# Hash-masked attention with a gated convolution: the sign products of heads 0 to 3 issued before the first scores, head 1 cast and stacked at once, one remainder of head 0 on GpSimd

## The chip, the cores and the metric

The kernel runs on one core of one Trainium2 chip. The metric is the device time of one execution in microseconds (us). Before the change the median of three runs is 633.61 us (633.21 to 634.43).

## The reference

```python
q_bits = (q @ proj > 0)                    # 6 bits for every row of q, and of k
k_bits = (k @ proj > 0)
q_bucket, k_bucket = sum(bits * 2**arange(6))
scores = where(q_bucket == k_bucket, q @ k.T / sqrt(D), -1e9)
attn = exp(scores - max(scores))           # per row
attn = attn / (sum(attn) + 1e-9)
x = (attn @ v), heads side by side         # B=4, H=8, S=768, D=64 -> (4, 768, 512)
gate = sigmoid(causal depthwise conv of x, 5 taps)
out = (gate * (x @ w_val)) @ w_out         # w: 512 x 512, given as float64
```

Batch 4, 8 heads, 768 rows, head dimension 64. The output is 4 x 768 x 512 in fp32.

## The kernel before

A *unit* is one of the 32 pairs of batch and head ("head i" below, heads 0 to 31 in order). A *tile* `k` is one block of 128 query rows of a head, six to a head, 192 in all; so tiles 0 to 5 belong to head 0, tiles 6 to 11 to head 1.

**Stacks.** fp32 products are made from parts that are rounded to fp32r. For each head there are four arrays: `aq` and `ak` (rounded q and k in rows 0 to 63, and in rows 64 to 75 the twelve sign rows that make the mask), `bq` and `bk` (128 rows that hold rounded values and remainders). `scores(k)` multiplies `ak` by `aq` and then `bk` by `bq` into one PSUM tile `s` (two halves of 384 columns, so four matmuls, L232). There are two `s` tiles, so `scores(k)` waits until `exponentials(k-2)` on ScalarE (ACT) has read its tile.

**Where the stacks come from.** The raw q and k of a head lie in `r` (`load_raw`, L147, five buffers). Head 0 goes a short way, `first_prep`: sign products into a PSUM tile `tp` (L211), casts on ACT and VectorE (DVE) (L213, L214, L215, L223), one remainder on GpSimd (POOL; L216: `bk`) and one on DVE (L217: `bq`), then four small evictions of the sign products on DVE (L219). All later heads go through `prep(i)`: GpSimd casts `aq` (L166) and subtracts for the remainder `bq` (L168); DMAs on SyncE's queue (SP) copy the rows to where they belong (L169 to L172) and the sign rows from a tile `u` (L174, L175). `u` holds the sign rows of four heads. `bits(i)` makes it in two halves: four small matmuls side by side in the columns of the array into a PSUM tile `m` (L194; one matmul for each of four heads, `raws[i + jj]`), and an eviction on DVE (L197). For heads 0 to 3 that is `first_bits`, a generator that is stepped, ahead of `prep(1)`, inside the main loop.

**The main loop** goes over `k`. In each turn stand, in this order: copies of the transposed probabilities of tile `k-4` out of PSUM (ACT, L289), `maxima(k)` (DVE, L238), small DVE steps (L244, L248, L262, L266), `normalise(k-2)` (GpSimd, L271), `scores(k+1)` (TensorE, PE), `exponentials(k)` (ACT, L256), steps of generators that run beside it (the preparation of the weights L90 to L112, the stacks `preps`, attention times v L303, the feed-forward part), and `transposes(k-3)` (PE, L280). Before the loop `scores(0)` is issued.

**What sets the order.** PE, ACT, DVE and GpSimd issue in the order in which the code is written (`manual_schedule`). The DMAs on SP are placed by a scheduler, and each waits on SP for what it needs, so a DMA that waits holds up those behind it. [...]

Of the kernel before, what the change touches and what calls it, by code (L numbers as in the profile page):

```python
# [8 lines left out]
FP32 = mybir.dt.float32  # L9
FP32R = mybir.dt.float32r  # L10
AF = mybir.ActivationFunctionType
ALU = mybir.AluOpType
# [14 lines left out]
def kernel(  # L27
# [10 lines left out]
    nc = tc.nc  # L38
    B, H, _, S = qk.shape
    P = 128  # L40
    D = 64
    KB = S // P
    HS = S // 2
# [9 lines left out]
    stk = ctx.enter_context(tc.tile_pool(name="stk", bufs=2))  # L53
# [9 lines left out]
    op = ctx.enter_context(tc.tile_pool(name="op", bufs=2))  # L63
# [3 lines left out]
    ps_v = ctx.enter_context(tc.tile_pool(name="ps_v", bufs=1, space=PSUM))  # L67
    ps_m = ctx.enter_context(tc.tile_pool(name="ps_m", bufs=1, space=PSUM))
# [5 lines left out]
    rows_sb = packed[:, 64:68]  # L74
    proj_sb = const.tile([P, 32], FP32, name="proj_sb")
# [67 lines left out]
    def load_raw(i):  # L143
        if i < len(units):
            b, h = units[i]
            raws[i] = raw.tile([P, S], FP32, name="r")
            nc.sync.dma_start(out=raws[i], in_=qk[b, h])  # L147

    def load_values(i):
        b, h = units[i]  # L150
        if h % 2 == 0:
            vts[i] = vp.tile([P, KB, P], FP32, name="vt")
            nc.sync.dma_start(out=vts[i], in_=v[b, h // 2])
        else:
            vts[i] = vts[i - 1]

    def prep(i):

        if i >= len(units):
            return  # L160
        b, h = units[i]
        j = h % 4
        load_values(i)
        r = raws[i]
        aq, ak, bq, bk = stacks[i] = [stk.tile([P, S], FP32R, name=nm) for nm in ("aq", "ak", "bq", "bk")]
        nc.gpsimd.tensor_copy(out=aq, in_=r)  # L166
        yield
        nc.gpsimd.tensor_tensor(out=bq, in0=r, in1=aq.bitcast(FP32), op=ALU.subtract)  # L168
        nc.sync.dma_start(out=ak[0:D].bitcast(FP32), in_=aq[D:P].bitcast(FP32))  # L169
        nc.sync.dma_start(out=bk[0:D].bitcast(FP32), in_=aq[D:P].bitcast(FP32))  # L170
        nc.sync.dma_start(out=bk[D:P].bitcast(FP32), in_=bq[D:P].bitcast(FP32))
        nc.sync.dma_start(out=bq[D:P].bitcast(FP32), in_=aq[0:D].bitcast(FP32))  # L172
        u = cur["u"]
        nc.sync.dma_start(out=aq[D:M].bitcast(FP32), in_=u[32 * j:32 * j + 2 * NB].bitcast(FP32))  # L174
        nc.sync.dma_start(out=ak[D:M].bitcast(FP32), in_=u[32 * j + 2 * NB:32 * j + 4 * NB].bitcast(FP32))  # L175
        load_raw(i + 5)
        if j == 3 and i + 1 < len(units):
            yield
            yield from bits(i + 1)

    def side_tile():
        if not moes:
            return ps_m.tile([P, 512], FP32, name="m")
        return ps_t.tile([P, 512], FP32, name="tp")

    def bits(i):

        u = stk.tile([P, S], FP32R, name="u", bufs=2)
        for hf in range(2):
            yield  # L190
            sl = slice(hf * HS, (hf + 1) * HS)
            z = side_tile()
            for jj in range(4):
                nc.tensor.matmul(out=z[32 * jj:32 * jj + 32, 0:HS], lhsT=proj_sb,  # L194
                                 rhs=raws[i + jj][:, sl], start=True, stop=True,
                                 tile_position=(0, 32 * jj))
            nc.vector.tensor_scalar(out=u[:, sl], in0=z[:, 0:HS], scalar1=rows_sb[:, 0:1], scalar2=rows_sb[:, 1:2],  # L197
                                    op0=ALU.is_ge, op1=ALU.mult)
        cur["u"] = u

    def first_bits():
        yield from bits(0)
        load_raw(5)

    def first_prep():

        r = raws[0]
        aq, ak, bq, bk = stacks[0] = [stk.tile([P, S], FP32R, name=nm) for nm in ("aq", "ak", "bq", "bk")]
        z = ps_t.tile([P, 512], FP32, name="tp")
        for g in range(4):  # L210
            nc.tensor.matmul(out=z[32 * g:32 * g + 2 * NB, 0:HS], lhsT=proj_sb[:, 2 * NB * (g // 2):2 * NB * (g // 2 + 1)],  # L211
                             rhs=r[:, HS * (g % 2):HS * (g % 2 + 1)], start=True, stop=True, tile_position=(0, 32 * g))
        nc.scalar.copy(out=aq[0:D], in_=r[0:D])  # L213
        nc.vector.tensor_copy(out=bk[D:P], in_=r[D:P])  # L214
        nc.vector.tensor_copy(out=ak[0:D], in_=r[D:P])  # L215
        nc.gpsimd.tensor_tensor(out=bk[0:D], in0=r[D:P], in1=bk[D:P].bitcast(FP32), op=ALU.subtract)  # L216
        nc.vector.tensor_tensor(out=bq[D:P], in0=r[0:D], in1=aq[0:D].bitcast(FP32), op=ALU.subtract)  # L217
        for g in (0, 2, 3, 1):
            nc.vector.tensor_scalar(out=(aq, ak)[g // 2][D:M, HS * (g % 2):HS * (g % 2 + 1)],  # L219
                                    in0=z[32 * g:32 * g + 2 * NB, 0:HS],  # L220
                                    scalar1=rows_sb[32 * g:32 * g + 2 * NB, 2:3],
                                    scalar2=rows_sb[32 * g:32 * g + 2 * NB, 3:4], op0=ALU.is_ge, op1=ALU.mult)
        nc.scalar.copy(out=bq[0:D], in_=r[0:D])  # L223

    def scores(k):
        i, qt = tiles[k]
        aq, ak, bq, bk = stacks[i]
        qs = slice(qt * P, (qt + 1) * P)
        s = ss[k] = ps_s.tile([P, 2, 512], FP32, name="s")
        for lq, rk, n in ((aq, ak, M), (bq, bk, P)):  # L230
            for hf in range(2):
                nc.tensor.matmul(out=s[:, hf, 0:HS], lhsT=lq[0:n, qs],  # L232
                                 rhs=rk[0:n, hf * HS:(hf + 1) * HS], start=n == M, stop=n == P)

    def maxima(k):
        s = ss[k]
        nm = small.tile([P, 1], FP32, name="nm")
        nc.vector.tensor_reduce(out=nm, in_=s[:, :, 0:HS], axis=AX.XY, op=ALU.max, negate=True)  # L238
        nms[k] = nm
# [182 lines left out]
    tiles = [(i, qt) for i in range(len(units)) for qt in range(KB)]  # L422

    raws, stacks, vts, ss, nbs, ps, tps, sums, rcs, nms, gs, cur = {}, {}, {}, {}, {}, {}, {}, {}, {}, {}, {}, {}
    avs, convs, moes = [], [], []
    accs = [(ps_m, "m")]

    def step(gens):

        while gens:  # L430
            try:
                return next(gens[0])
            except StopIteration:
                gens.pop(0)

    def finish(gens):
        while gens:
            step(gens)
# [3 lines left out]
    with tc.manual_schedule(engines=ENGINES):  # L442
        for i in range(5):
            load_raw(i)
        load_values(0)
        first_prep()
        weights = [[load_conv(), load_weights(0)], [load_weights(1)]]
        preps = [first_bits(), prep(1)]
        scores(0)
        step(weights[0])  # L450
        step(weights[1])
        turn = 0
        for k in range(N + LAG + 1):
            if 0 <= k - LAG - 1:
                keep_transposed(k - LAG - 1)
            pair = k % 2 == 0 and 0 <= k - 2 < N
            if k < N:
                maxima(k)
            if pair:
                row_sums(k - 2)  # L460
            if k < N:
                factors(k)
            if pair:
                recip(k - 2)
            if 0 <= k - 2 < N:
                normalise(k - 2)
            if k < N:
                shifts(k)
            if k + 1 < N:
                if tiles[k + 1][0] != tiles[k][0]:  # L470
                    finish(preps)
                    preps = [prep(tiles[k + 1][0] + 1)]
                scores(k + 1)
            if k < N:
                exponentials(k)
            if k >= 60 or k % 2:
                step(convs)
            for _ in range((1, 0, 2, 0, 2, 2)[k % 6]):
                step(weights[turn])
                turn = 1 - turn  # L480
            for _ in range(3 if cur["gates"] else 1):
                step(moes)
            cur["gates"] = max(0, cur["gates"] - 1)
            step(preps)
            if k % 2:
                step(avs)
                step(avs)
            if 0 <= k - LAG < N:
                transposes(k - LAG)
        accs[:] = [(ps_m, "m"), (ps_t, "tp"), (ps_s, "s"), (ps_t, "tp"), (ps_s, "s")]  # L490
        finish(avs)
        cur["gates"] = 0
        cur["end"] = True
        while convs:
            step(convs)
            step(moes)
        finish(moes)
# [59 lines left out]
```

## Time and profile before

| what | value |
|---|---|
| median of three runs | 633.61 us (633.21 to 634.43) |
| span of the profiled execution, from first to last instruction | 633.2 us |
| PE busy | 591.4 us (93%) |
| DVE busy | 451.3 us (71%) |
| ACT busy | 421.1 us (67%) |
| POOL busy | 386.0 us (61%) |
| mean granted TensorE clock | 0.986 |

The profile counts its times from the span's start; the median of the runs lies 0.4 us above that span. "Busy" counts every instruction of an engine; idle time of an engine that no one waits for costs nothing. In a timeline row stand: start in us, duration in us, engine, line, operation, written tile <- read tiles, shapes, how many instructions were merged, and in brackets the idle time just before and what ended it. "SPq" is a DMA being issued from SP; its transfer ends later.

### The profile page before, as it was taken

The page shows a single profiled execution, that of the slowest core. Times are in us where ns is not written, and L with a number is a line of the kernel's source. Part 1 is how long each engine was busy: PE and PEld are TensorE (multiplying, and loading weights), DVE is VectorE, ACT ScalarE, POOL GpSimd, SP SyncE. Part 2 cuts the span into 40 slices and gives each one's busy share as a digit, 9 for nine tenths or more (in the row PEclk, how much of TensorE's full clock was granted, in tenths as well). Part 3 has the DMA queues.
Part 4 walks back from the last instruction along what each step waited for, and adds up shares of the span by engine and source line. Part 5 has one row for each costly group of instructions (what it writes and reads, how often), then busy time and mean ns, then how long its engine had stood idle before and what let it go on. Part 6 is the DMA issues. An engine that isn't in the chain of part 4 may idle for free.

```text
span 633.2 us, 10639 instructions
## 1 busy us (share of the span) xinstructions
PE 591.4 (93%) x3496; PEld 426.2 (67%) x3496; DVE 451.3 (71%) x1033; ACT 421.1 (67%) x881; POOL 386.0 (61%) x357
## 2 busy tenths in 40 slices
PE   3699888989999999999999999999999999999997
PEld 2476555546667777676657777677667777776895
DVE  5689798999885856668675867668584786665532
ACT  3487777768778676667787776667778667675400
POOL 1476877778966765467754776467663677544221
PEclk9889997989999999999999999999999999999999
DMA  6533534443433334243333234243422223300111
GB/s 244 131 83 92 152 95 139 112 126 91 106 79 80 72 77 122 72 103 97 105 80 93 74 80 122 70 122 81 122 55 61 56 55 81 85 18 2 50 51 50
DMA packets 23270, 56.77 MB, mean 90 GB/s; under 512 B 4296, under 2 KB 4296, under 8 KB 23216
## 3 DMA queue, kind: packets, MB, share of 16 engines
q1 hardware_dynamic: 23072, 56.06, 33.3%
q8 instruction: 28, 0.46, 0.3%
q14 instruction: 26, 0.21, 0.1%
q10 hardware_dynamic: 144, 0.03, 0.0%
HBM read 23.12 MB, written 6.29 MB: 46 GB/s over the span
## 4 chain that ended last, share of the span: by engine, by line
PE 69%; ACT 14%; DVE 12%; issue 2%; DMA 2%; POOL 0%; SPq 0%; ACTq 0%; POOLq 0%; DVEq 0%
PE av L303 19%; PE s L232 17%; PE tp L280 12%; PE m L390 8%; PE m L365 7%; ACT p L256 6%; ACT pt L289 4%; DVE nm L238 3%; ACT x L311 3%; PE tp L365 1%; PE tp L390 1%; PE s L390 1%; DVE u L197 1%; PE tp L194 1%; DVE g L334 1%
## 5 line engine op out<-in xcount | busy, mean ns | idle before, releaser
L271 POOL TENSOR_SCALAR p<-p,ri 128x768 f32<-128x768 f32 x192 | 215.9, 1129 | 173.8 <-DVE nb L248 149.6
L238 DVE TENSOR_REDUCE nm<-s 128x1 f32<-128x768 f32 x192 | 182.5, 951 | 64.3 <-PE s L232 64.2
L289 ACT COPY pt<-tp 128x384 f32<-128x384 f32 x384 | 166.1, 485 | 86.7 <-PE tp L280 85.8
L256 ACT ACTIVATE p<-s,nb,gs 128x768 f32<-128x768 f32 x192 | 192.4, 1002 | 47.0 <-DVE nb L248 41.1
L280 PEld LDWEIGHTS tp<-ident,p 128*128 128x128 f32 x1152 | 131.2, 142 | 73.2 <-issue 46.4
L280 PE MATMUL tp<-ident,p 128*128 128x128 f32 x1152 | 166.3, 281 | 3.8 <-DVE u L197 1.5
L303 PE MATMUL av<-pt,vt 128*64 128x384 f32 x768 | 147.6, 506 | 0.0
L232 PE MATMUL s<-ak,aq 76*128 76x384 f32 x384 | 119.5, 393 | 28.9 <-ACT p L256 24.7
L232 PE MATMUL s<-bk,bq 128*128 128x384 f32 x384 | 101.6, 346 | 0.0
L303 PEld LDWEIGHTS av<-pt,vt 128*64 128x64 f32 x768 | 47.6, 137 | 63.7 <-issue 63.1
L232 PEld LDWEIGHTS s<-ak,aq 76*128 76x128 f32 x384 | 59.9, 196 | 45.2 <-ACT p L256 38.0
L334 DVE SCALAR_TENSOR_TENSOR g<-x,cw_sb,g 128x768 f32<-128x768 f32 x64 | 77.9, 1217 | 0.2
L232 PEld LDWEIGHTS s<-bk,bq 128*128 128x128 f32 x384 | 72.4, 195 | 0.5 <-issue 0.5
L376 POOL TENSOR_TENSOR hl<-ht,hh 128x384 fp32r<-128x384 f32 x32 | 32.2, 1006 | 45.9 <-DVE hh L374 45.9
L168 POOL TENSOR_TENSOR bq<-r,aq 128x768 fp32r<-128x768 f32 x31 | 58.3, 1882 | 0.0
L311 ACT COPY x<-av 64x384 f32<-64x384 f32 x64 | 30.3, 474 | 33.8 <-PE av L303 33.2
L365 PE MATMUL m<-xh,wv 128*128 128x384 f32 x200 | 42.8, 338 | 0.0
L248 DVE TENSOR_SCALAR nb<-nm,gs 128x1 f32<-128x1 f32 x192 | 39.9, 208 | 3.5
L324 POOL TENSOR_TENSOR xl<-x,xh 128x384 fp32r<-128x384 f32 x32 | 33.5, 1062 | 12.3 <-DVE xh L323 12.3
L370 DVE TENSOR_TENSOR ht<-m,g 128x384 f32<-128x384 f32 x25 | 13.9, 555 | 35.4 <-PE m L365 32.0
L256 ACT ACTIVATION_READ_ACCUMULATOR p<-s,nb,gs 128x1 f32 x192 | 39.0, 203 | 0.0
L390 PE MATMUL m<-wo,hh 128*128 128x512 f32 x144 | 38.2, 395 | 0.0
(84 smaller groups left out, 487.4 us busy)
## 6 DMA issues: line engine op xcount, KB each, us to landing
r<-in_qk_dram SPq DMA_DIRECT2D x32, 384.0 KB
vt<-in_v_dram SPq DMA_DIRECT2D x16, 384.0 KB
out_dram<-o SPq DMA_DIRECT2D x24, 256.0 KB
ak<-aq SPq DMA_DIRECT2D x31, 192.0 KB
bk<-aq SPq DMA_DIRECT2D x31, 192.0 KB
bk<-bq SPq DMA_DIRECT2D x31, 192.0 KB
bq<-aq SPq DMA_DIRECT2D x31, 192.0 KB
w<-in_w_val_dram SPq DMA_DIRECT2D x4, 512.0 KB
```

The source lines that it names most:

```text
L168: nc.gpsimd.tensor_tensor(out=bq, in0=r, in1=aq.bitcast(FP32), op=ALU.subtract)
L232: nc.tensor.matmul(out=s[:, hf, 0:HS], lhsT=lq[0:n, qs], rhs=rk[0:n, hf * HS:(hf + 1) * HS], start=n == M, stop=n == P)
L238: nc.vector.tensor_reduce(out=nm, in_=s[:, :, 0:HS], axis=AX.XY, op=ALU.max, negate=True)
L256: nc.scalar.activation(out=p, in_=s[:, :, 0:HS], func=AF.Exp, bias=nb, scale=gs.pop(k), accum_out=sm[:, k % 2, 0:1])
L271: nc.gpsimd.tensor_scalar(out=p, in0=p, scalar1=rcs.pop(k), scalar2=1.0, op0=ALU.mult, op1=ALU.mult)
L280: nc.tensor.transpose(out=tp[:, n * P:(n + 1) * P], in_=p[:, kb * P:(kb + 1) * P], identity=ident)
L289: nc.scalar.copy(out=pt[:, :, qo:qo + P], in_=tp[:, 0:HS].rearrange("p (a b) -> p a b", b=P))
L303: nc.tensor.matmul(out=av[s * D:(s + 1) * D, 0:HS], lhsT=vt[:, kb, hh * D:(hh + 1) * D], rhs=pt[kb // 3][:, kb % 3, :], start=(kb == 0), s ...
L311: nc.scalar.copy(out=x[hh * D:(hh + 1) * D, o:o + HS], in_=av[s * D:(s + 1) * D, 0:HS])
L334: nc.vector.scalar_tensor_tensor(out=g, in0=x[:, k:k + S], scalar=w, in1=g, op0=ALU.mult, op1=ALU.add)
L365: nc.tensor.matmul(out=acc[:, 0:HS], lhsT=wv[wi][:, c, j * P:(j + 1) * P], rhs=xs_[(c, o)][xi], start=(m == 0), stop=(m == 11))
L390: nc.tensor.matmul(out=acc, lhsT=hs[(o, j)][hi][:, tb * P:(tb + 1) * P], rhs=wo[wi][:, j, :], start=(m == 0), stop=(m == 11))
```

## The change

The change has four parts, all in the first turns of the program.

1. `first_bits` is gone. `first_signs` issues the sign matmuls of heads 0 to 3 right behind `first_prep` and ahead of `scores(0)`: the first half into the `m` tile, the second into the `av` tile. Both are evicted into `u` later, by DVE, inside `prep(1)`.
2. `prep(1)` no longer pauses between its cast and its remainder, and its first step is taken before the loop: GpSimd does both for head 1 ahead of the first `normalise`, and four copying DMAs are released. The DMAs of the sign rows still come after both evictions into `u`.
3. The remainder `bq[D:P]` of head 0 is computed on GpSimd in place of DVE.
4. `load_raw(5)` stands right behind `scores(0)`.

```diff
@@ prep(i) @@
         nc.gpsimd.tensor_copy(out=aq, in_=r)
-        yield
+        if i > 1:
+            yield
         nc.gpsimd.tensor_tensor(out=bq, in0=r, in1=aq.bitcast(FP32), op=ALU.subtract)
         ...
+        if i == 1:
+            yield
+            yield
+            for hf, z in enumerate(zs):
+                sl = slice(hf * HS, (hf + 1) * HS)
+                nc.vector.tensor_scalar(out=cur["u"][:, sl], in0=z[:, 0:HS], scalar1=rows_sb[:, 0:1],
+                                        scalar2=rows_sb[:, 1:2], op0=ALU.is_ge, op1=ALU.mult)
+                yield
         u = cur["u"]
@@
-    def first_bits():
-        yield from bits(0)
-        load_raw(5)
+    def first_signs():
+        cur["u"] = stk.tile([P, S], FP32R, name="u", bufs=2)
+        for hf, (pool, name) in enumerate(((ps_m, "m"), (ps_v, "av"))):
+            z = pool.tile([P, 512], FP32, name=name)
+            for jj in range(4):
+                nc.tensor.matmul(out=z[32 * jj:32 * jj + 32, 0:HS], lhsT=proj_sb,
+                                 rhs=raws[jj][:, hf * HS:(hf + 1) * HS], start=True, stop=True,
+                                 tile_position=(0, 32 * jj))
+            zs.append(z)
@@ first_prep() @@
-        nc.vector.tensor_tensor(out=bq[D:P], in0=r[0:D], in1=aq[0:D].bitcast(FP32), op=ALU.subtract)
+        nc.gpsimd.tensor_tensor(out=bq[D:P], in0=r[0:D], in1=aq[0:D].bitcast(FP32), op=ALU.subtract)
@@ before the loop @@
-        preps = [first_bits(), prep(1)]
+        first_signs()
+        preps = [prep(1)]
+        step(preps)
         scores(0)
+        load_raw(5)
```

On PE, at the program's start, before (L211 head 0's signs, L232 scores, L194 the signs of heads 0 to 3):

```order
L211 MATMUL tp<-r,proj_sb 12x384 x4
L232 MATMUL s<-ak,aq 128x384 x2
L232 MATMUL s<-bk,bq 128x384 x2
L232 MATMUL s<-ak,aq 128x384 x2
L232 MATMUL s<-bk,bq 128x384 x2
L232 MATMUL s<-ak,aq 128x384 x2
L232 MATMUL s<-bk,bq 128x384 x2
L194 MATMUL m<-r,proj_sb 32x384 x4
L232 MATMUL s<-ak,aq 128x384 x2
L232 MATMUL s<-bk,bq 128x384 x2
L194 MATMUL m<-r,proj_sb 32x384 x4
```

The same place after (L226 head 0's signs, L215 the signs of heads 0 to 3, L247 scores):

```order
L226 MATMUL tp<-r,proj_sb 12x384 x4
L215 MATMUL m<-r,proj_sb 32x384 x4
L215 MATMUL av<-r,proj_sb 32x384 x4
L247 MATMUL s<-ak,aq 128x384 x2
L247 MATMUL s<-bk,bq 128x384 x2
L247 MATMUL s<-ak,aq 128x384 x2
L247 MATMUL s<-bk,bq 128x384 x2
L247 MATMUL s<-ak,aq 128x384 x2
```

The two groups of sign matmuls moved from behind the scores of tiles 2 and 3 to the place ahead of those of tile 0; from the scores of tile 4 on PE's order is that of before.

On GpSimd, from the first remainder on, before (L216 and L168 remainders, L166 the cast of the next head, L271 normalising):

```order
L216 TENSOR_TENSOR bk<-r,bk 64x768
L271 TENSOR_SCALAR p<-p,ri 128x768
L166 CAST aq<-r 128x768
L271 TENSOR_SCALAR p<-p,ri 128x768
L168 TENSOR_TENSOR bq<-r,aq 128x768
L271 TENSOR_SCALAR p<-p,ri 128x768 x2
L166 CAST aq<-r 128x768
```

The same place after (L231 and L232 both remainders of head 0, L166 and L169 head 1, L286 normalising):

```order
L231 TENSOR_TENSOR bk<-r,bk 64x768
L232 TENSOR_TENSOR bq<-r,aq 64x768
L166 CAST aq<-r 128x768
L169 TENSOR_TENSOR bq<-r,aq 128x768
L286 TENSOR_SCALAR p<-p,ri 128x768 x4
L166 CAST aq<-r 128x768
```

Head 1's cast and remainder no longer stand between the normalisings of tiles 0, 1 and 2.

On SP, from behind the first weight's load on, before (L153 and L136 loads of v and of a weight, L147 raw loads, L169 to L175 the copies into the stacks of heads 1 and 2):

```order
L153 DMA vt<-in_v_dram 128x768
L136 DMA w_423<-in_w_val_dram 128x1024
L147 DMA r<-in_qk_dram 128x768
L175 DMA ak<-u 12x768
L169 DMA ak<-aq 64x768
L170 DMA bk<-aq 64x768
L171 DMA bk<-bq 64x768
L147 DMA r<-in_qk_dram 128x768
L174 DMA aq<-u 12x768
L172 DMA bq<-aq 64x768
L169 DMA ak<-aq 64x768
```

The same place after (L170 to L173 the copies out of `aq` and `bq`, L183 and L184 those out of `u`):

```order
L147 DMA r<-in_qk_dram 128x768
L170 DMA ak<-aq 64x768
L171 DMA bk<-aq 64x768
L172 DMA bk<-bq 64x768
L147 DMA r<-in_qk_dram 128x768
L183 DMA aq<-u 12x768
L173 DMA bq<-aq 64x768
L184 DMA ak<-u 12x768
L153 DMA vt<-in_v_dram 128x768
L170 DMA ak<-aq 64x768
L171 DMA bk<-aq 64x768
L184 DMA ak<-u 12x768
```

The copies of head 1 no longer stand behind `ak<-u`; the two that read `u` and `bq<-aq` now stand together behind both raw loads; the load of v and of the second weight (`w_423`, further down) moved behind head 1's copies. From head 2's `bk<-bq` on, SP has the order of before, and so have all engines from about tile 5 on. On DVE only the remainder L217 is gone; the two evictions into `u` stand where they stood, behind the small steps of tile 1 and behind those of tile 2.

More of the change, by code (lines that the diff above doesn't have):

```diff
@@ L424 @@
     raws, stacks, vts, ss, nbs, ps, tps, sums, rcs, nms, gs, cur = {}, {}, {}, {}, {}, {}, {}, {}, {}, {}, {}, {}
-    avs, convs, moes = [], [], []
+    avs, convs, moes, zs = [], [], [], []
     accs = [(ps_m, "m")]
```

## The prediction, made before the changed kernel ran

> **What bounds the kernel now.** I read the page first: PE is busy for nearly the whole span, and the chain that ended last lies mostly on it. So a microsecond that the start loses is not made up later; the question is what the start loses.
>
> ```profile
> span 633.2 us, 10639 instructions
> PE 591.4 (93%) x3496; PEld 426.2 (67%) x3496; DVE 451.3 (71%) x1033; ACT 421.1 (67%) x881; POOL 386.0 (61%) x357
> PE 69%; ACT 14%; DVE 12%; issue 2%; DMA 2%; POOL 0%; SPq 0%; ACTq 0%; POOLq 0%; DVEq 0%
> ```
>
> Then the timeline of the first 31 us.
>
> ```profile
> 4.11 0.83 ACT L213 CAST aq<-r 64x768 fp32r<-64x768 f32 x1 [1.66 <-DMA r<-in_qk_dram]
> 4.57 1.48 PE L211 MATMUL tp<-r,proj_sb 128*12 128x384 f32 x8 [4.57 <-DVE proj_sb L76]
> 5.19 0.52 SPq L136 DMA_DIRECT2D w<-in_w_val_dram  x1
> 5.24 2.11 POOL L216 TENSOR_TENSOR bk<-r,bk 64x768 fp32r<-64x768 f32 x1 [3.94 <-DVE bk L214]
> 5.70 2.46 DVE L217 TENSOR_TENSOR bq<-r,aq 64x768 fp32r<-64x768 f32 x1
> 8.09 0.66 DVE L219 TENSOR_SCALAR aq<-tp,packed 12x384 fp32r<-12x384 f32 x1
> 9.59 1.32 PE L232 MATMUL s<-ak,aq 76*128 76x384 f32 x2 [3.54 <-DVE ak L219]
> 10.70 0.84 PE L232 MATMUL s<-bk,bq 128*128 128x384 f32 x2
> 11.58 0.96 DVE L238 TENSOR_REDUCE nm<-s 128x1 f32<-128x768 f32 x1 [0.72 <-PE s L232]
> 13.08 0.99 ACT L256 ACTIVATE p<-s,nb,gs 128x768 f32<-128x768 f32 x1 [7.30 <-DVE nb L248]
> 14.21 1.01 PE L232 MATMUL s<-ak,aq 76*128 76x384 f32 x2 [1.39 <-ACT p L256]
> 15.79 1.51 PE L194 MATMUL m<-r,proj_sb 128*32 128x384 f32 x8
> 17.45 0.68 DVE L197 TENSOR_SCALAR u<-m,packed 128x384 fp32r<-128x384 f32 x1 [3.17 <-PE m L194]
> 18.04 0.95 DVE L238 TENSOR_REDUCE nm<-s 128x1 f32<-128x768 f32 x1
> 18.51 0.85 PE L194 MATMUL m<-r,proj_sb 128*32 128x384 f32 x8
> 20.31 0.67 DVE L197 TENSOR_SCALAR u<-m,packed 128x384 fp32r<-128x384 f32 x1
> 20.32 0.82 POOL L166 CAST aq<-r 128x768 fp32r<-128x768 f32 x1
> 20.65 0.62 PE L232 MATMUL s<-ak,aq 76*128 76x384 f32 x2 [1.29 <-ACT p L256]
> 21.11 0.51 PE L232 MATMUL s<-bk,bq 128*128 128x384 f32 x2
> 21.98 1.81 POOL L168 TENSOR_TENSOR bq<-r,aq 128x768 fp32r<-128x768 f32 x1
> 24.22 0.99 ACT L256 ACTIVATE p<-s,nb,gs 128x768 f32<-128x768 f32 x1
> 25.57 0.80 SPq L174 DMA_DIRECT2D aq<-u  x1
> 26.70 0.48 SPq L172 DMA_DIRECT2D bq<-aq  x1
> 27.73 0.18 DVE L100 SCALAR_TENSOR_TENSOR cw<-cw,cwt 128x20 f32<-128x20 uint32 x1
> 28.54 0.98 PE L232 MATMUL s<-ak,aq 76*128 76x384 f32 x2 [3.40 <-ACT p L256]
> 29.54 0.98 PE L232 MATMUL s<-bk,bq 128*128 128x384 f32 x2
> 30.56 0.96 DVE L238 TENSOR_REDUCE nm<-s 128x1 f32<-128x768 f32 x1 [2.65 <-PE s L232]
> ```
>
> Three losses are seen. Head 0's first scores start at 9.59, when DVE, which had been held by the subtraction L217 for 2.46 us, has made the sign rows. DVE then stands idle for 3.17 us until 17.45: the eviction into `u` is queued ahead of `maxima(2)`, and its matmuls ran only at 15.79, behind the scores of tile 2. And PE stands idle for 3.40 us until 28.54. That row names ACT, but `exponentials(4)` had ended at 25.2; the scores of tile 6 are the first to read head 1's stack, and the rows of SP show `aq<-u` issued at 25.57 and `bq<-aq` at 26.70, 2.97 and 2.84 us ahead of the two starts 28.54 and 29.54. So this wait is for DMAs. Behind it PE is slow for 6 us:
>
> ```profile
> 25.00:28.50 3.50, 0.13 (x2) 0.98 0.82 220
> 28.50:31.60 3.10, 3.04 (x11) 0.50 0.64 156
> 31.60:34.80 3.20, 3.20 (x14) 0.50 0.01 3
> ```
>
> (stretch, its length, PE busy, granted clock, DMA share, GB/s): the granted clock falls to 0.50, and two matmuls of one pass take 0.98 us in place of 0.62 and 0.51.
>
> **The change part by part.**
>
> *The first scores.* DVE loses the 2.46 us of L217, so its evictions can begin when the tp matmuls are done (4.57 + 1.48 = 6.05); two of 0.66 give `scores(0)` what it needs at 7.4, where before it was 9.45. PE is then not free: the sixteen sign passes stand ahead. They need the raw loads of heads 1 to 3, whose landing no row shows. The DMA view up to 6.5 us bounds it:
>
> ```profile
> q1 hardware_dynamic: 568, 1.58, 65.2%
> q1 hardware_dynamic: 837, 2.33, 73.5%
> ```
>
> By 6.5 us SP's queue had moved 1.58 MB, four raw loads of 0.393 MB; by 8.3 us (second row) 2.33 MB, all five and most of the next. The first landed at 4.11. If loads finish in the order of issue the fourth is there at about 7.0 (an estimate, 0.5 us behind its last byte, as for the first); 8.8 is the late end. Eight passes took 1.51 us at 15.79 and 0.85 us at 18.51, four heads side by side, so two passes in a row are 1.51 or 0.85. From 7.0 the fourth head has four in a row: 1.7 to 3.0 us, PE free at 8.7 to 10.0; I take 9.4, since PE has been at work from 4.57 and the slow rows are those near a start. `scores(0)` then takes 1.13 us (the pair at 20.65) to 1.97 (9.59 to 11.56; of it 0.3 was waiting). With 1.8 I get its end at 11.2, before 11.54: 0.35 gained, ends -0.1 and 1.7. The other input is `bq` from GpSimd: L216 ends at about 7.3, a second such subtraction at 1.66 to 2.11 ends at 9.0 to 9.5, ahead of PE's second pair at about 10.2. It costs nothing while the sign passes cover it; alone it would be late against 7.4 + 1.3, by 0.8 at most.
>
> [...]
>
> *DVE's wait.* The eviction into `u` finds its matmuls long done and runs in the gap between the maxima of tiles 1 and 2. `maxima(2)` now waits for `scores(2)` alone, which needs `exponentials(0)`: in before that ended 2.53 us behind the end of `scores(0)`, PE started 0.13 later, and a quadruple of matmuls takes 1.13 to 1.65. So `maxima(2)` starts 3.8 to 4.3 us behind the end of `scores(0)`; before it was 18.04 - 11.54 = 6.5. Gain 2.2 to 2.7; I take 2.6, as PE has by then been busy for long. From 18.04 to 27.91 DVE had hardly an idle moment in before, and its order is unchanged, so the gain of 2.95 so far stands for all of that stretch. GpSimd's cast and remainder (0.82 and 1.81) run at about 9 to 12, where GpSimd stood idle, and leave the row between the normalisings: nothing waits for them there.
>
> *Head 1's stack.* The second eviction ended at 20.98, now at about 18.05. On SP `aq<-u` waits for it, with `bq<-aq` and `ak<-u` queued behind; all else of head 1 was issued by about 12, with both raw loads. Issues of 0.8, 0.5 and 0.8 us and 2.9 to landing give a complete stack at about 22.5. `scores(6)` can start when `exponentials(4)` is done, 25.3 - 2.95 = 22.4, and needs 1.13; DVE asks for it at 27.91 - 2.95 = 25.0. So the wait vanishes with 1.3 us to spare, and PE does not idle into the half clock. What is late next is DVE (tile 6 and 7 carry weight preparation) and then ACT:
>
> ```profile
> 32.32 1.28 DVE L100 SCALAR_TENSOR_TENSOR w<-w,o 128x512 f32<-128x512 uint32 x1
> 33.52 0.94 DVE L238 TENSOR_REDUCE nm<-s 128x1 f32<-128x768 f32 x1
> 35.52 0.96 DVE L238 TENSOR_REDUCE nm<-s 128x1 f32<-128x768 f32 x1 [0.62 <-PE s L232]
> 38.15 0.62 PE L232 MATMUL s<-ak,aq 76*128 76x384 f32 x2 [0.39 <-ACT p L256]
> 42.81 0.68 ACT L90 ACTIVATE o<-w 128x512 f32<-128x512 f32 x1
> ```
>
> On the time axis of before (less the 2.95), `maxima(6)` starts at 27.91 in place of 30.56 (2.65 earlier). Behind it stand 0.45 of small steps, 0.42 and 1.28 of weights: `maxima(7)` at about 31.1, not 33.52 (2.4). `maxima(8)` follows at 32.4 for 35.52 (3.1), and from there exponentials and two PSUM copies (0.99 + 0.19 + 0.85) pace the tiles: `scores(10)` at about 35.65 for 38.15. So 2.5 more, ends 2.2 and 3.1.
>
> *What was moved behind.* The second weight's load goes from 5.19 to about 26 and is read at 42.81, now about 37.4: covered by 11 us. The load of v for heads 2 and 3 is read later still. `load_raw(5)` comes earlier and is needed only by the next sign products. Head 2's stack hangs on GpSimd's `normalise(4)`, which moves with tile 6: free.
>
> *Sum.* 0.35 + 2.6 + 2.5 = 5.45 off the span of 633.2, hence 627.75; with the 0.4 between that span and the median 633.61, 628.2.
>
> **The rivals.**
>
> *The stack is not earlier relative to DVE.* If the three DMAs behind the second eviction again take the 7.5 us from 20.98 to 28.5, the idle of PE and the half clock stay. Only 2.95 is gained: 630.7. For it speaks that SP holds them in a row behind one wait; against it, that in before they also waited for GpSimd's L168 until 23.8 and had raw loads between them, which are gone by then.
>
> *PE is fast early.* Full rate from about 7 on ends `scores(0)` at 9.85: 1.7 + 2.65 + 2.5 = 6.85, 626.7.
>
> *The gain is lost again.* If tiles behind 10 wait for something that keeps its own time, it is 633.6. The chain has no such thing: loads and weights wait for buffers that the same tiles free.
>
> *Slower.* The fourth raw load holds PE's queue: `scores(0)` stands behind it, and everything behind that. Each microsecond of landing past 7.0 costs one; the 5.45 are used up at 12.4, and at 13.7 the time is 634.9. The DMA rows speak against it: the bytes were moved by 6.5.
>
> *The change does not do what it says* only if the scheduler had kept SP's order, and the order of the built program shows that it did not.
>
> **How the numbers follow.** Likeliest, as summed, 0.72, own range 626.9 to 629.5; PE fast early 0.10; stack late 0.11; lost again 0.04; slower 0.03. The low end takes in most of the fast rival, the high end most of the late stack: 626.4 to 630.6 leaves out less than 0.2. A change of 0.2%, 1.27 us, is about what a measurement tells from none: faster by more than that 0.92, within it 0.05, slower 0.03.
>
> **What the profile would show.** Right: sign passes from 6 to about 9.5; `maxima(2)` at about 15 without a wait for the sign matmuls; no idle of 3 us on PE before `scores(6)` and no clock of 0.50 there; `scores(10)` near 32.7. Wrong: the first maximum later than 12, or PE waiting for head 1's DMAs again, or a shift that is smaller at the end than at 40 us.

## The result, and the profile after

The changed kernel took 628.69 us (median of 4 runs, 627.65 to 630.86) against 634.02 before: a ratio of 0.9923, 95% interval 0.9906 to 0.9940. Run again beside its parts it took 630.06 (627.13 to 631.98) against 633.64: 0.9942, 0.9921 to 0.9963. So it is faster, by 3.6 to 5.3 us (under 1%), and its runs lie much further apart (4.9 us) than those of the kernel before on the same chip (2.1 us). The spread is half of the story.

The page of the changed kernel, for the lines shown of before:

```profile
span 627.4 us, 10639 instructions
PE 591.0 (94%) x3496; PEld 425.8 (68%) x3496; DVE 448.6 (72%) x1032; ACT 421.2 (67%) x881; POOL 388.2 (62%) x358
PE 68%; DVE 13%; ACT 12%; DMA 3%; issue 2%; POOL 1%; SPq 0%; ACTq 0%; POOLq 0%; DVEq 0%
```

Its timeline, the rows that answer to those shown of before (L215 sign passes, L232 GpSimd's second remainder, L247 scores, L253 maxima, L179 evictions into `u`, L183 and L184 the copies out of `u`):

```profile
7.48 0.13 PEld L215 LDWEIGHTS m<-r,proj_sb 128*32 128x32 f32 x1 [1.10 <-DMA r<-in_qk_dram]
7.55 1.80 POOL L232 TENSOR_TENSOR bq<-r,aq 64x768 fp32r<-64x768 f32 x1
8.12 1.46 PE L215 MATMUL av<-r,proj_sb 128*32 128x384 f32 x5
9.51 0.62 PE L247 MATMUL s<-ak,aq 76*128 76x384 f32 x2
9.97 0.51 PE L247 MATMUL s<-bk,bq 128*128 128x384 f32 x2
10.52 0.96 DVE L253 TENSOR_REDUCE nm<-s 128x1 f32<-128x768 f32 x1 [1.51 <-PE s L247]
12.02 0.99 ACT L271 ACTIVATE p<-s,nb,gs 128x768 f32<-128x768 f32 x1 [6.09 <-DVE nb L263]
13.13 0.67 DVE L179 TENSOR_SCALAR u<-m,packed 128x384 fp32r<-128x384 f32 x1
13.15 0.62 PE L247 MATMUL s<-ak,aq 76*128 76x384 f32 x2 [1.96 <-ACT p L271]
14.16 0.96 DVE L253 TENSOR_REDUCE nm<-s 128x1 f32<-128x768 f32 x1 [0.36 <-PE s L247]
16.42 0.67 DVE L179 TENSOR_SCALAR u<-av,packed 128x384 fp32r<-128x384 f32 x1
16.79 1.01 PE L247 MATMUL s<-ak,aq 76*128 76x384 f32 x2 [1.38 <-ACT p L271]
17.12 0.86 SPq L183 DMA_DIRECT2D aq<-u  x1
18.63 0.78 SPq L184 DMA_DIRECT2D ak<-u  x1
22.20 0.70 PE L247 MATMUL s<-ak,aq 76*128 76x384 f32 x2
23.79 0.95 DVE L253 TENSOR_REDUCE nm<-s 128x1 f32<-128x768 f32 x1
29.36 1.01 PE L247 MATMUL s<-ak,aq 76*128 76x384 f32 x2 [1.32 <-ACT p L271]
31.94 0.93 PE L247 MATMUL s<-ak,aq 76*128 76x384 f32 x2
```

The fourth raw load let PE go on at 7.48, the sign passes ended at 9.6, and the first scores went at full rate (0.62 and 0.51 us a pair, where before it was 1.32, with 0.3 of waiting in it, and 0.84). `maxima(2)` starts at 14.16 with 0.36 us of waiting, not at 18.04. The scores of tile 6 start at 22.20 with no idle before them, where before PE stood for 3.40 us. Two rows show something that was not forecast: at 16.79 and at 29.36 a pair takes 1.01 us, although PE had been idle for no more than 1.38 and 1.32 us just before.

Where the time came from is read best from the starts of `exponentials(k)` in the three timelines, with the lead over the profile of before in brackets:

```
tile    before   changed          changed + fillers (below)
0        13.08    12.02 (1.06)     11.46 (1.62)
2        19.52    15.66 (3.86)     15.08 (4.44)
5        27.00    22.96 (4.04)     22.38 (4.62)
6        32.21    25.28 (6.93)     24.70 (7.51)
8        37.01    29.94 (7.07)     29.36 (7.65)
10       41.83    35.92 (5.91)     34.19 (7.64)
18       62.59    56.70 (5.89)     54.95 (7.64)
40      124.99   119.19 (5.80)    116.17 (8.82)
184     554.10   548.37 (5.73)    545.04 (9.06)
```

Three steps up: 1.06 by the first exponential, 2.80 by tile 2, 2.9 at tile 6. Then a step down of 1.16 between tiles 8 and 10. From tile 40 to the end the lead of the changed kernel stays within 0.1 us. (A run's time is 1.8 us longer than its span: 629.21 to 627.4 for this one. So the profile of before, span 633.2, is of an execution of about 635, one of its longer ones; the leads against it are about 1.4 us more than against a median of 633.6.)

The step down has its row in the windows view (stretch, length, PE busy, granted clock, DMA share, GB/s):

```profile
12.20:15.60 3.40, 1.94 (x8) 1.00 0.92 224
15.60:22.40 6.80, 5.61 (x21) 0.50 0.42 116
22.40:25.80 3.40, 3.15 (x21) 1.00 0.47 101
25.80:29.30 3.50, 1.63 (x10) 0.99 0.64 177
29.30:32.70 3.40, 3.34 (x12) 0.50 0.74 190
87.30:90.70 3.40, 1.53 (x12) 1.00 0.42 92
90.70:97.50 6.80, 6.33 (x21) 0.50 0.35 74
```

In this profile the stretches in which PE was busy for 1.94, 1.63 and 1.53 us of 3.40 to 3.50 are followed by 6.80, 3.40 and 6.80 us at half the clock. That became the second theory.

### The profile page after: what moved, and what is told of

Same layout as the page of the kernel before. It is cut to its first block, busy times and chain, and to the rows that moved or that the text cites. A ratio compares the mean times of both kernels' runs of the same rounds, so it can differ in the third digit from the quotient of the medians.

```text
span 627.4 us, 10639 instructions
## 1 busy us (share of the span) xinstructions
PE 591.0 (94%) x3496; PEld 425.8 (68%) x3496; DVE 448.6 (72%) x1032; ACT 421.2 (67%) x881; POOL 388.2 (62%) x358
## 4 chain that ended last, share of the span: by engine, by line
PE 68%; DVE 13%; ACT 12%; DMA 3%; issue 2%; POOL 1%; SPq 0%; ACTq 0%; POOLq 0%; DVEq 0%
PE av L318 18%; PE s L247 16%; PE tp L295 12%; PE m L405 8%; PE m L380 7%; ACT p L271 5%; DVE nm L253 4%; ACT pt L304 4%; ACT x L326 2%; PE tp L380 1%; PE tp L405 1%; PE s L405 1%; DVE g L349 1%; DVE o L93 1%; PE tp L203 1%
## 5 line engine op out<-in xcount | busy, mean ns | idle before, releaser
L286 POOL TENSOR_SCALAR p<-p,ri 128x768 f32<-128x768 f32 x192 | 216.6, 1132 | 165.8 <-DVE nb L263 141.6
L253 DVE TENSOR_REDUCE nm<-s 128x1 f32<-128x768 f32 x192 | 182.5, 951 | 63.5 <-PE s L247 63.3
L271 ACT ACTIVATE p<-s,nb,gs 128x768 f32<-128x768 f32 x192 | 192.7, 1003 | 43.2 <-DVE nb L263 40.2
L247 PE MATMUL s<-ak,aq 76*128 76x384 f32 x384 | 118.1, 389 | 23.9 <-ACT p L271 23.2
L247 PE MATMUL s<-bk,bq 128*128 128x384 f32 x384 | 100.6, 343 | 0.0
L247 PEld LDWEIGHTS s<-ak,aq 76*128 76x128 f32 x384 | 59.2, 194 | 38.0 <-ACT p L271 36.8
L247 PEld LDWEIGHTS s<-bk,bq 128*128 128x128 f32 x384 | 71.6, 193 | 0.0
L169 POOL TENSOR_TENSOR bq<-r,aq 128x768 fp32r<-128x768 f32 x31 | 58.0, 1871 | 0.1
L271 ACT ACTIVATION_READ_ACCUMULATOR p<-s,nb,gs 128x1 f32 x192 | 39.1, 204 | 0.0
```

Source lines behind the costliest of these rows:

```text
L247: nc.tensor.matmul(out=s[:, hf, 0:HS], lhsT=lq[0:n, qs], rhs=rk[0:n, hf * HS:(hf + 1) * HS], start=n == M, stop=n == P)
L271: nc.scalar.activation(out=p, in_=s[:, :, 0:HS], func=AF.Exp, bias=nb, scale=gs.pop(k), accum_out=sm[:, k % 2, 0:1])
L286: nc.gpsimd.tensor_scalar(out=p, in0=p, scalar1=rcs.pop(k), scalar2=1.0, op0=ALU.mult, op1=ALU.mult)
```

## The experiments

Two theories stood against each other. **Waits**: the change takes away three waits in a row and the rest of the program moves with them. **Clock**: what counts is whether PE is at full rate. Each kernel was timed in five rounds beside the kernel before; the last column gives the mean granted clock of its runs. That mean takes the time ahead of the first entry of the clock's record as full rate; in e3 (below) the pairs there took 0.98 to 1.01 us, as long as at a recorded 0.50.

| run | median us | before | less | ratio, 95% | clock |
|---|---|---|---|---|---|
| e1 whole change | 630.06 | 633.64 | 3.6 | 0.9921 to 0.9963 | 0.981 to 0.992 |
| e2 part 1 alone | 630.24 | 633.64 | 3.4 | 0.9930 to 0.9958 | 0.984 to 0.992 |
| e3 parts 2, 3 alone | 629.78 | 633.64 | 3.9 | 0.9925 to 0.9950 | 0.991 to 1.000 |
| e4 whole but part 3 | 629.34 | 633.64 | 4.3 | 0.9908 to 0.9949 | 0.980 to 0.995 |
| e5 signs behind tile 1 | 627.77 | 633.80 | 6.0 | 0.9887 to 0.9918 | 0.988 to 0.991 |
| e6 whole + fillers | 626.64 | 633.80 | 7.2 | 0.9868 to 0.9903 | 0.993 to 0.997 |
| e7 + late fillers | 626.87 | 633.80 | 6.9 | 0.9864 to 0.9898 | 0.996 to 1.000 |
| e8 before + fillers | 632.57 | 633.26 | 0.7 | 0.9972 to 0.9997 | 0.986 to 0.997 |
| e9 part 1 + fillers | 630.26 | 633.26 | 3.0 | 0.9938 to 0.9969 | 0.990 to 0.997 |
| e10 parts 2, 3 + fillers | 629.53 | 633.26 | 3.7 | 0.9920 to 0.9949 | 0.991 to 0.993 |
| e11 = e6 again | 627.16 | 633.26 | 6.1 | 0.9881 to 0.9915 | 0.993 to 0.994 |
| e12 = e6 but part 3 | 626.38 | 633.39 | 7.0 | 0.9874 to 0.9910 | 0.993 to 1.000 |

**The parts.** e1 is the changed kernel. e2 is the kernel before with `first_signs` and two late evictions:

```diff
-        yield from bits(0)
+        for hf, z in enumerate(zs):
+            yield
+            nc.vector.tensor_scalar(out=cur["u"][:, sl], in0=z[:, 0:HS], ...)
         load_raw(5)
...
+        first_signs()
         preps = [first_bits(), prep(1)]
```

e3 is the changed kernel with the sign matmuls issued in `prep(1)`, just ahead of each eviction; e4 has L232 on `nc.vector` again.

> The changed kernel itself, for the comparison with the parts. Both theories: 5.3 to 5.9 us below the kernel before. Theory 'waits': the change took away three waits that stood in a row (first scores 1.0, DVE's wait for the sign matmuls 2.8, PE's wait for head 1's stack about 3, of which 1 is given back). Rival 'clock': what counts is that PE works early and without a break, so that it is at full rate in the first 30 us; the waits themselves are side effects.

> Part 1 alone: sign products ahead of the first scores, evicted by DVE in the same places; head 1's cast and remainder between the normalisings as before, bq's remainder on DVE. Waits: DVE's subtraction holds the first scores at about 9.5, their end comes 0.8 earlier because PE is at full rate; DVE's wait goes (2.8); head 1's copies still come late, so PE's idle of about 3 us before the scores of tile 6 stays: 3.6 us gained in all. Clock: PE is busy as early as in the whole change, so most of it is gained, 5 or more.

> Parts 2 and 3 without part 1: head 1 cast and stacked at once and bq's remainder on GpSimd, but the sign matmuls stand where they stood before (behind the scores of tiles 2 and 3). Waits: first scores 1.2 earlier (they wait for GpSimd's second remainder at about 9.4), DVE's wait of about 3 us stays, head 1's stack is in time (2.5): 3.7 us gained. Clock: PE idles from 6 to 9.4 and is slow longer than in the whole change: 1 us gained at most.

> The whole change but part 3: bq's remainder of head 0 stays on DVE. Waits: the sign matmuls hold PE until 9.5 anyway, and DVE's sign rows are ready at about 9.5 too, so at most 0.2 us of the gain is lost. Rival: the first scores are DVE's business and part 3 carries the 1.06 us that the first exponential gained; then 0.8 to 1.5 us are lost against the whole change.

e2 (3.4) and e3 (3.9) came out as "waits" said, 3.6 and 3.7, and not as "clock" did. e3 is the plainest case: its record of the clock begins at 26.5 us, and the first pair of matmuls of each of tiles 2 to 6, ahead of that, takes 0.98 to 1.01 us, that of tiles 7 and 8, behind it, 0.59 and 0.62. So by these pairs e3 ran at half rate up to 26.5 us and gained 3.9 us all the same. And the changed kernel is faster than the kernel before at a lower recorded clock (e1's runs 0.981 to 0.992, those before beside them 0.988 to 1.000). But the whole, at 3.6, was no better than either half, which "waits" cannot have: it had asked for 5.3 to 5.9. The profile of e1 is of its fastest run, 627.13. It is the same program as the first profile, and its half-rate stretch at 14.6 is not followed by a second:

```profile
11.20:14.60 3.40, 1.57 (x7) 1.00 0.93 242
14.60:21.40 6.80, 5.63 (x21) 0.50 0.53 138
24.90:28.30 3.40, 2.01 (x14) 1.00 0.82 211
28.30:31.70 3.40, 2.66 (x16) 1.00 0.62 151
```

Its lead at tile 8 is 7.50 and at tile 10 still 7.50, where the first profile fell from 7.07 to 5.91. So one and the same program lost 1.16 us in one run and nothing in the other: from 25.80 to 29.30 PE was busy for 1.63 of 3.50 us in the one and 0.50 followed, from 24.90 to 28.30 for 2.01 of 3.40 in the other and 1.00 followed. Another 0.44 of the 2.1 us between the two runs was there at the first exponential (11.58 for 12.02), and some 0.6 came later. No profile shows the slowest run, 631.98. The e4 run, 4.3, spread over 626.79 to 630.95: too far to price part 3.

**Holding the clock.** e5 moves the real sign passes into PE's idle time behind the scores of tile 1. e6 puts small matmuls that nobody reads into three idle places; e7 into two more, at 88 and 125 us, where DVE is late with weights and gate.

```diff
+    def filler(r, pool, name, n):
+        z = pool.tile([P, 512], FP32, name=name)
+        for jj in range(n):
+            g = 32 * (jj % 4)
+            nc.tensor.matmul(out=z[g:g + 32, 0:HS], lhsT=proj_sb, rhs=r[:, 0:HS],
+                             start=True, stop=True, tile_position=(0, g))
...                                          # at the end of turn k
+            if k in (0, 2, 6):               # e7: 30 and 42 too, six each
+                filler(raws[tiles[k][0] + 2], *((ps_t, "tp", 6), (ps_m, "m", 6), (ps_m, "m", 4))[...])
```

> The whole change, but the sixteen sign passes stand behind the scores of tile 1, where PE idles from 11.2 to 13.2 us, in place of ahead of those of tile 0; raw load 5 right behind them. Theory 'waits': the first scores end at about 10, when GpSimd's second remainder is there (9.4), so up to 0.5 us earlier than in the changed kernel; the sign passes end before the scores of tile 2 are released, and the rest moves with it: 0 to 0.5 us better than the changed kernel. [...]

> The whole change, and small matmuls that nobody reads (6, 6 and 4 of 32 columns by 384, on PE alone) at the ends of turns 0, 2 and 6, where PE idles 1.3 to 2.0 us. [...] Waits alone: the fillers stand in idle time and change nothing, or cost up to 0.5.

> As the run with fillers in turns 0, 2 and 6, and six small matmuls each at the ends of turns 30 and 42 too, where PE idles 2.4 us because DVE is late (weights and gate in one turn) and where the profiles show a half-rate stretch of 3.4 to 6.8 us behind it. Clock: hardly any half-rate stretch is left before the end, the mean granted clock is 0.995 or more, the runs lie closer together than those of the changed kernel (a spread of under 2 us in place of 4.9), and the median is 1.5 to 3 us below that of the changed kernel. Waits alone: no change against the changed kernel, the same spread.

e6 took 626.64 us and its runs lie within 1.4 us of each other. Sixteen matmuls that nobody reads made the changed kernel faster. None of its stretches from 7.6 to 31.5 us is at half rate; in the least busy one PE has 2.09 of 3.40 us. Three of them, and the later place that was left alone:

```profile
11.00:14.40 3.40, 2.52 (x19) 1.00 0.88 249
17.80:21.20 3.40, 2.09 (x13) 1.00 0.72 168
28.10:31.50 3.40, 2.60 (x16) 1.00 0.62 146
86.10:89.50 3.40, 1.07 (x9) 1.00 0.55 119
89.50:92.90 3.40, 3.40 (x12) 0.50 0.11 26
```

By waits alone e6 should have gained nothing over e1. It gained 3.4 us (by medians that were not taken side by side), more than the 1.16 us of the one step down that I had a price for. Five of e1's six runs have a clock of 0.981 to 0.983, against 0.992 for the one profiled: by an estimate from these, 11 to 14 us more at half rate, but no profile of e1 shows where. In the table above the lead of e6 does not fall between tiles 8 and 10. The stretch at 15 us cost nothing: with it e1 led by 4.47 at tile 5, without it e6 by 4.62, of which 0.12 was there at the first exponential; DVE is the fuller engine there (in the first profile busy for 6.41 of the 6.80 us from 15.60, PE for 5.61).

e7 is a miss in part. Its clock is 1.000 in two runs, but its median is that of e6 and its runs spread over 2.4 us. Between tiles 30 and 40 it gained 1.44 us on the kernel before, which stands at half rate for 6.83 us there. e6, with one stretch of 3.41, gained 1.27, and the changed kernel of the first profile, with 6.83 us too, 0.04. So, an estimate from these three, one late stretch of 3.41 us at half rate costs about 0.2 us in that place, and a second one behind it 1.2 (e1, with one too, gained only 0.53 there). What the profile of e7 lacks against that of e6 was missing from the first exponential on (12.79 for 11.46). e5 gave 627.77, 6.0 below, with runs within 1.0 us: real work in an idle place does most of what the fillers do, and more than the 0 to 0.5 that waits allowed it (2.3 over e1, by medians that were not taken side by side). Its first exponential came at 11.76, between e1's 11.58 and the 12.02 of the first profile, so not from earlier first scores.

**The parts with fillers.** e8, e9 and e10 are the kernel before, part 1 and parts 2 and 3 with fillers in their idle places (turns 0, 2 and 6; e8 and e9 turn 4 too). e11 repeats e6, e12 is e6 with L232 on `nc.vector`.

> The kernel before, with unread small matmuls (4, 6, 8 and 4) at the ends of turns 0, 2, 4 and 6, where it idles. It asks whether the fillers gain by themselves, without the change. Theory 'waits and clock': the three waits stay, only the half-rate stretch behind the wait for head 1's stack is gone, so 0.5 to 1.5 us below the kernel before, far from the 7 of the changed kernel with fillers. Rival 'it is all clock': 3 us or more.

> Part 1 alone, with fillers at turns 0, 2, 4 and 6, so that the clock is held and the waits are priced without it. Waits: first scores and DVE's wait, 1.2 + 2.8 = 4.0 us below the kernel before; PE still waits about 3 us for head 1's stack ahead of the scores of tile 6. Rival (part 2 is not needed once the clock is held): 6 to 7, as in the whole change with fillers.

> Parts 2 and 3 without part 1, with fillers at turns 0, 2 and 6. Waits: first scores 1.2 and head 1's stack 2.8 earlier, DVE's wait of about 3 stays: 4.0 us below the kernel before. Rival (the early sign products count only because they keep PE busy): 6 to 7, as in the whole change with fillers.

> The whole change with fillers at turns 0, 2 and 6 once more, on the chip of these runs: 6.5 to 7.5 us below the kernel before, and the sum of its parts: about 1.2 for the first scores, 2.8 for DVE's wait, 2.9 for head 1's stack.

> The whole change with fillers at turns 0, 2 and 6, but bq's remainder of head 0 stays on DVE: the price of part 3 with the clock held. Theory: the sixteen sign passes hold PE until about 9.5 us, and DVE's sign rows would be ready then too, so the first maximum comes 0 to 0.3 us later at the same clock, and the median stays 6 to 7 us below the kernel before. Rival: part 3 carries the first microsecond; 5 to 5.5 below.

Fillers alone bring the kernel before 0.7 us, in runs that lie 4.0 us apart. They did not hold its clock: its profile stands at half rate from 27.1 to 34.0 us, behind the wait for head 1's stack, and its runs show no higher clock than those before. So it is e3, and not e8, that tells against "all clock". With fillers the halves bring 3.0 and 3.7 and the whole 6.1 to 7.2, about their sum (e11, at 6.1, is less than expected); without, all three brought 3.4 to 3.9. That is what both theories together say, and neither alone.

The steps of the lead over the profile of before price the two waits in all profiles. From tile 0 to tile 2 the lead grows by 2.74 to 2.82 in eight of the nine that have the sign matmuls ahead of the first scores (2.13 in e4, at half rate from 13.6 us); in e3 and e10, which leave them where they stood, by 0.00 and -0.23. From tile 5 to tile 6 it grows by 2.76 to 2.91 in all ten that cast and stack head 1 at once; in e2 and e9, which do not, by 0.19 and -1.66. The second step is nearly the same at half rate (e3, 2.76) and at full rate (e6, 2.89). e10 still shows the wait that it left in, before the eviction into `u`, and e9 the one that it left in, before the scores of tile 6:

```profile
16.34 0.68 DVE L184 TENSOR_SCALAR u<-m,packed 128x384 fp32r<-128x384 f32 x1 [3.39 <-PE m L181]
```

```profile
22.27 0.80 SPq L174 DMA_DIRECT2D aq<-u  x1
27.28 0.93 PE L253 MATMUL s<-ak,aq 76*128 76x384 f32 x2 [4.03 <-issue]
```

In this profile of e9 the copies of the stack took 5.0 us from the issue of `aq<-u`, not the 2.97 of before, and half rate follows (27.3 to 30.7 us). It is of the run of 632.28, 1.4 to 2.2 us longer than the other five, so it does not say why the median brought 3.0 and not 4.0. The first exponential led by 0.51 in it, where 1.2 was expected, and by 0.58 in e2, which has the same start: that is most of what is missing. Why those DMAs were slower in this run I did not settle.

e12 prices part 3 by its median: 626.38, no slower than e6. The subtraction is as slow on DVE as before, and in this profile the scores start when the sign passes are done, not later:

```profile
5.61 2.45 DVE L239 TENSOR_TENSOR bq<-r,aq 64x768 fp32r<-64x768 f32 x1
7.86 2.12 PE L215 MATMUL av<-r,proj_sb 128*32 128x384 f32 x5
9.91 0.81 PE L254 MATMUL s<-ak,aq 76*128 76x384 f32 x2
```

But full rate came only at 10.3 us in this run, so the sign passes were late too. In e2, which has the subtraction on DVE as well, it came at 7.6, and PE waited for DVE's sign rows twice:

```profile
9.55 0.41 PE L246 MATMUL s<-ak,aq 76*128 76x384 f32 x1 [0.71 <-DVE ak L233]
10.18 0.44 PE L246 MATMUL s<-ak,aq 76*128 76x384 f32 x1 [0.21 <-DVE ak L233]
```

The first exponential of e2 came at 12.50, that of e6, with full rate from 7.6 too, at 11.46. In e12 it came at 12.59, in e11 and e7, with full rate from 10.1 and 10.4, at 12.75 and 12.79. So by these profiles part 3 gains about 1 us where full rate comes at 7.6 and nothing where it comes at 10; the medians of e6, e11 and e12 do not tell it from nothing. The best version of the study is the change with fillers, e6 and e12.

## Why the prediction was right, and where it was not

The predicted 628.2 lies 0.5 below the first median and 1.9 below the second; both lie in the range (626.4 to 630.6), though three of the ten single runs (up to 631.98) do not. The forecast is the median before, 633.61, less the gain of 5.45; the 0.4 in its sum is not the distance from a run's span to its time, which is 1.8.

*First scores*: forecast 0.35, measured 1.06 in the first profile. The step that failed there is the rate at which `scores(0)` runs. Landing (7.48 for 7.0) and the end of the sign passes (9.6 for 9.4) were near, and the fast rival came true in part: all four matmuls ran in 0.97 us, for which I had taken 1.8. I took the granted clock of 1.00 in the early rows of before for the rate at which PE ran. That was a misreading: the record of the clock starts only at 18.1 us in that profile (8.8 in the changed one), and the view shows 1.00 ahead of it. The pairs there (1.01 us at 14.21, 1.00 at 17.23) are as long as those at a recorded 0.50 later (0.98 at 28.54, 0.99 at 31.45), and behind 18.1 the pair at 20.65 takes 0.62. That PE is quick once it has been at work for long, the reason given for two of the choices in the sum, was an estimate; no run shows a time for it, and with one start full rate came anywhere from 7.59 to 10.38 us.

Nor is 1.06 the size of this step. Five profiles have the same program up to the first exponential, and the fourth raw load lands at 7.5 to 7.7 us in all of them; what differs is the first entry of the clock's record, here called full rate (behind it the first pairs of the changed kernel take 0.62 and 0.51 us):

```
profile    full rate from   sign passes end   first exponential (lead)
e6              7.59             9.03              11.46 (1.62)
e1              7.79             9.14              11.58 (1.50)
changed         8.78             9.58              12.02 (1.06)
e11            10.08            10.32              12.75 (0.33)
e7             10.38            10.30              12.79 (0.29)
```

So the forecast of 0.35 is what two runs show and the fast rival's 1.7 nearly what two others show. The prediction took for one value what changes from run to run with the clock, and which of them the first profile met was luck.

*DVE's wait*: forecast 2.6, measured 2.80.

*Head 1's stack*: forecast 2.5 at tile 10. At tile 6 it was 2.9 (for 2.65), and the copies of `u` went out on SP between 17.12 and 19.4, in the spacing worked out; with fillers it stays at 3.0 (e6: 7.64 less 4.62). In the changed kernel 1.16 of it is given back at 29 us. The step that failed is the sentence that PE does not idle into the half clock. I had looked for one long idle and took its absence for safety; the stretch ahead of 29.3 us has no idle above 1.32 us, PE was busy for 1.63 of 3.50 us in it, and 0.50 followed. Nor was the time ahead of the scores of tile 6 free of the half clock, as the prediction had said it would be: it stood at 0.50 from 15.6 to 22.4, which by the leads cost nothing.

*Sum and what hides*: 5.45 against 5.8 by the spans, and 5.3 and 3.6 by the two medians. A loss that was not forecast and a first term that was too small stood against each other, so that the first median came within 0.5 us is in part luck. The moved loads cost nothing, as said: the lead is constant beyond tile 40.

*The rivals*: "lost again" did not come as a wait, but the half clock takes back 0.8 to 3.6 us, an estimate from the gains without and with fillers (3.6 and 5.3 against 6.1 to 7.2 in e6, e11 and e12). The stack was not late, and the fourth load held PE for 1.1 us and no more. GpSimd's remainder was covered by the sign passes, as said (it ends at 9.35, they at 9.6); DVE's would have been too in a run like that of e12, and not in one like that of e2.

## What to carry to other kernels

Follow a start-up tile by tile with one instruction that every tile has (here the exponential's start): each wait is a step, and a step that comes back down is a cost the sum has missed. When waits are removed near the start, look at the granted clock and at the length of the pairs behind every gap, not only at the longest idle: here 0.50 followed a stretch without an idle above 1.32 us. Real work moved into the gaps (e5) and a few unread matmuls (e6) gave medians 2.3 and 3.4 us below e1's, where a part of the change alone gave 3.4 to 3.9. And where one program's runs spread by several us, halves and whole cannot be compared until that cause is held. One profile shows one run: the first step here was 0.29 to 1.62 us in five profiles of one start.

## What the runs showed of the hardware

In the fourteen profiles the record of the clock begins between 7.6 us (e2, e6) and 26.5 (e3). A mean clock over the time ahead of that reads 1.00, while the pairs of matmuls there are as long as at half rate: 0.98 to 1.01 us in e3, against 0.59 and 0.62 behind the first entry; 1.01 (at 14.21) in the profile of before, whose record begins at 18.1, against 0.62 (at 20.65). The half-rate stretches recorded in the body of the run are 6.83, 6.83 and 3.41 us long before (from 28.3, 96.6 and 134.1) and 6.83, 3.41, 6.83 and 3.41 in the changed kernel's first profile (from 15.6, 29.3, 90.7 and 128.2). In the 3.4 to 3.5 us ahead of each, PE was busy for 0.23, 1.39 and 1.02 us before and for 1.94, 1.63, 1.53 and 1.03 in the changed kernel. In the changed kernel no idle longer than 1.96 us (the row at 13.15) lay in or reached into the stretch ahead of the half rate at 15.6, and none longer than 1.32 us (the row at 29.36) that ahead of 29.3. Whether the clock follows the busy share, the idle times or something else, and at what value, is not shown: no run varied one of them alone.
